# A new written-out order for TensorE's work and for the projections in the first block of a two-block attention kernel

## The chip, the cores and the metric

The kernel runs on one core of one Trainium2 chip. The metric is the device time of one execution in microseconds (us). The kernel before was timed in three runs: 1796.18, 1799.53 and 1802.74 us, median 1799.53. One execution was also taken with the hardware profiler, and every row below is from that one.

## What is computed

Two independent attention blocks, A and B, each with its own input, weights and output projection; the outputs are laid side by side. Each has 2048 tokens, width 512 and 32 heads of 16. Block A lets a token see only itself and the 255 before it; block B sees all tokens. All in float32.

```python
qkv = (x @ wqkv).reshape(B, S, 3, H, Dh)          # S=2048, D=512, H=32, Dh=16
scores = einsum("bhqd,bhkd->bhqk", q, k) * Dh ** -0.5
# block A only: keep 0 <= query - key < 256
p = softmax(scores)
o = einsum("bhqk,bhkd->bhqd", p, v) @ wo
# result: concatenate([A, B], axis=-1)
```

## The kernel before

The heads of a block are taken in 8 groups of 4, and the queries in 4 chunks of 512, so a block has 32 units (group, chunk). The two groups of a pair share a set of projected rows. For each unit the kernel finds each query's maximum score first (line 518 in block A, line 471 in block B), puts the negated maxima, split into three rounded parts, beside the queries as extra rows of the contraction, and then computes scores from which the maximum is already subtracted (line 628). ScalarE takes the exponential (line 635), GpSimd cuts the window's triangles in block A (line 645), and TensorE sums the weighted values (line 674 in block A, line 659 in block B). Sums of the weights come from a column of ones beside the values.

In the first block all 96 projections are done too: q and k of both blocks (4 pairs x 4 chunks each), and v (16 tiles of 128 tokens per block). A projection is 12 matmuls: 4 slices of the contraction, each in 3 products of a value that is split into a high and a low part. A q or k projection goes from PSUM through a buffer `st` (two of them) to DRAM (`parts`), line 324, and is loaded back by four DMAs per chunk as `oq` (line 398) or `opk` (line 382). A v projection goes through `vst` to `vd` in DRAM and back into `vt` (line 434). All these DMAs are issued by SyncE's queue (SP) in the order in which the program was written. PSUM has seven banks for all of the first block's products (one more holds the weighted sums): a projection takes one, a maximum two neighbouring ones, a score step two.

The program is laid out once, in Python, by a loop that reads a string of letters, `ORDER_A`, one letter for one piece of TensorE's work, in the order in which TensorE then executes them:

- `p`: the next projection of the list `ORDER_P`, 12 matmuls over all 128 rows of the array (line 222).
- `g`: a quarter of the next two projections of that list, their contraction cut into halves that run in two halves of the array, 12 matmuls (line 352). Four `g` make two projections.
- `m`: one item of a unit's maxima, two heads, two matmuls (line 518); in block A VectorE follows with a masked copy (line 527) and a reduction (line 528), or for the first two tiles of the sequence with two masked reductions (line 523). Eight items make a unit.
- `t`: two transposes (line 595) that bring a unit's maxima into rows; ScalarE copies them out (`ntr`, line 597), and two DMAs put them beside the queries (line 602).
- `s`: scores of one step of a unit for two heads (line 628), two exponentials. A unit has six.
- `w`: the weighted values of a step (line 674). A unit has three.
- `e`: an item of the second block's maxima that is done early (line 471).

`ORDER_P` names the projections: block, kind, and two digits; for q and k these are pair and chunk (`Aq02` is block A's queries, pair 0, chunk 2), for v they are chunk and tile of 128 in it (`Av13`). Model times in the loop decide where DMA issues and VectorE's and ScalarE's follow-up work are put between the letters; the letters themselves are never reordered. Loads of the input have conditions on how many projections have been begun (`nb`). After the last letter the second block is written by other code, with its own repeated pattern; that is not touched.

Of the kernel before, what the change touches and what calls it, by code (L numbers as in the profile page):

```python
# [48 lines left out]
FILL = 16  # L49
WARM = 22  # L50
ORDER_P = (
# [4 lines left out]
    "Bq20 Bq12 Bk30 Bk31 Bk10 Bq33 Bq30 Bq31 Bk32 Bq32 Bk33 Bk21 ").split()  # L56
WAKE = 200
GAP_V = 1500
PIECE = 4
# [4 lines left out]


ORDER_A = (
    "pppppppppppmmmmpmmgmgmptmgmgmmpmsgmsgmmpmsgmsgmwtsmgmsgmmpmsgsmgmtwwmmmpsmgmsgmswwmsgmsgmmpmssptwsmg"
    "msgmswsmgsmgmmwwmgmsgmstwmsgmsgmmwtsgmsgmswmsgmsgmswmmmpssmtwwmspmsmwssmgsmgmswtmsgsmgmwsmswssmwmmmp"
    "mtmswmsswmsmpsmmpsmwtmmmpsmswmmspmsmwsmsmwwtmsmsmsmpmsmtwsmsmwsmmswssmwmmspmmswsmwtsmgmsgmswsmgsmtgm"
    "mwsmwsmmswsmsmpsmmwmswtmsmwsmmmpmsssmmwsmsmwtmmmpsmswmsmsmwtsmsmwsmmpmmswsmtwmmmpmsgmsgmswtsmgmswpsm"  # L70
    "gsmwwmsgmmgmpmsgmsgsmwwtsmgmsgmswsmgsmgmmwtsgsmgsmwwmsgmsgmgsmgmswsmgmmgmwsmwtmsgmsgmswtmsgsmgmswwsm"
    "gmsgmswsmgsmgsmtwwmmmpmsmpmsmwsmmswtmsgmsgmswsmgsmgsmwmsmtwsmmswssmwmmmpmssmtwswmmmpmsgsmgsmwwmsgsmg"
    "etwmmmpmsgmsgmswsegsmgegesgmswsmgesgemtwmmpmsmwmswmsgsmgestwmsgesgmmpemmpmsmwwtemmpsmgmsgsmwmgegsewm"
    "mmpesstwmgmsgeswsmgsmgsmwesgsmgsmwmgsmgmswesmpsmmwtwmmmpmmmwp")
LAND = 400
LAND_V = 0
LGAP = 2500
# [1189 lines left out]
```

## Time and profile before

| | |
|---|---|
| runs | 1796.18, 1799.53, 1802.74 us (median 1799.53) |
| profiled execution, its span from first to last instruction | 1797.4 us; no other time of that execution is listed |
| TensorE (PE) busy | 1779.1 us, 99% |
| VectorE (DVE) busy | 1510.2 us, 84% |
| ScalarE (ACT) busy | 1401.6 us, 78% |
| GpSimd (POOL) busy | 651.4 us, 36% |
| first block (all letters) | 0 to about 520 us |
| second block | about 520 to 1797 us |

Times in the rows are microseconds unless marked ns. PE is TensorE's matmul side. L222 is line 222 of the kernel. Matmuls are pipelined and their ends are modelled, so the distance between the starts of two rows tells more than a row's length. In a timeline row, `x12` is the number of instructions merged, and the bracket gives idle time of the engine just before and what ended it. SPq is SyncE's queue, where a row is the issue of DMAs, not their transfer.

### The profile page before, as it was taken

How to read it: one execution, taken by the hardware profiler on the slowest of the kernel's cores; microseconds unless marked ns; L12 is line 12 of the kernel's file. 1: busy time of each engine (PE TensorE's matmuls, PEld its weight loads, DVE VectorE, ACT ScalarE, POOL GpSimd, SP SyncE). 2: the span in 40 equal slices, each digit the busy share in tenths (PEclk: the TensorE clock that was granted, in tenths of full speed). 3: DMA queues.
4: the chain of work that ended last, by engine and by line, in shares of the span. 5: the costliest groups of instructions: out<-in, count | busy, mean ns of one | idle time of the engine just before them, and what ended most of it. 6: DMA issues, size and time to landing. Idle time of an engine off the chain costs nothing.

```text
span 1797.4 us, 39182 instructions
## 1 busy us (share of the span) xinstructions
PE 1779.1 (99%) x15054; PEld 907.9 (51%) x15054; DVE 1510.2 (84%) x2244; ACT 1401.6 (78%) x2749; POOL 651.4 (36%) x1334
## 2 busy tenths in 40 slices
PE   8999999999999999999999999999999999999999
PEld 6776657767754555444444444444444444444336
DVE  4766786676789677899999999999999999999911
ACT  4366676665569677899999999999999999999983
POOL 0377888656755331133400024220112422022220
PEclk9999999999999999999999999999999999999999
DMA  7766667645562223211200310130031121010012
GB/s 256 204 204 202 202 203 224 177 143 172 187 183 87 78 86 100 52 41 37 65 17 31 72 34 29 38 70 16 17 77 35 29 64 37 17 54 9 32 37 94
DMA packets 129354, 166.80 MB, mean 93 GB/s; under 512 B 23204, under 2 KB 59044, under 8 KB 129156
## 3 DMA queue, kind: packets, MB, share of 16 engines
q1 hardware_dynamic: 129168, 164.31, 31.0%
q8 instruction: 118, 1.93, 0.4%
q14 instruction: 68, 0.56, 0.1%
HBM read 94.49 MB, written 68.19 MB: 91 GB/s over the span
## 4 chain that ended last, share of the span: by engine, by line
PE 94%; DMA 2%; ACT 1%; DVE 1%; SPq 1%; issue 1%; POOL 0%; ACTq 0%; DVEq 0%
PE ps_all L659 30%; PE ps_all L471 20%; PE ps_all L628 19%; PE ps_all L222 11%; PE ps_all L352 7%; PE ps_all L674 4%; PE ps_all L518 3%; ACT p L635 1%; DMA in<-xT_A 1%; SPq L382 0%; PE ps_all L595 0%; DVE nm L528 0%; DMA in<-xT_B 0%; DVE ps_all L527 0%; DMA vd<-vst 0%
## 5 line engine op out<-in xcount | busy, mean ns | idle before, releaser
L635 ACT ACTIVATE p<-ps_all 128x512 f32<-128x512 f32 x2432 | 1260.9, 597 | 178.8 <-PE ps_all L628 114.6
L475 DVE TENSOR_REDUCE mt<-ps_all 128x2 f32<-128x1024 f32 x1516 | 1195.6, 870 | 63.0 <-PE ps_all L471 63.0
L628 PE MATMUL ps_all<-oq,opk 51*128 51x512 f32 (+2 forms) x2752 | 768.4, 404 | 4.5 <-ACT p L635 2.4
L471 PE MATMUL ps_all<-opk,oq 48*128 48x512 f32 x2016 | 673.3, 438 | 0.2
L659 PE MATMUL ps_all<-p,vt 128*17 128x256 f32 (+1 forms) x6056 | 586.2, 460 | 1.7 <-ACT ou L685 1.7
L628 PEld LDWEIGHTS ps_all<-oq,opk 51*128 51x128 f32 x2752 | 394.6, 185 | 179.0 <-ACT p L635 150.3
L471 PEld LDWEIGHTS ps_all<-opk,oq 48*128 48x128 f32 x2016 | 307.7, 184 | 315.3 <-DVE mt L475 179.5
L645 POOL TENSOR_SCALAR_AFFINE_SELECT p<-p 128x256 f32<-128x256 f32 x480 | 179.8, 409 | 110.7 <-ACT p L635 108.8
L659 PEld LDWEIGHTS ps_all<-p,vt 128*17 128x17 f32 x6056 | 101.5, 95 | 228.1 <-issue 215.7
L545 POOL TENSOR_TENSOR mu<-mt 128x16 f32<-128x16 f32 x31 | 6.9, 221 | 509.3 <-DVE mt L475 509.3
L527 DVE COPY_PREDICATED ps_all<-mone,ps_all 128x256 f32<-128x256 uint16 x224 | 95.3, 426 | 82.0 <-PE ps_all L518 75.4
L528 DVE TENSOR_REDUCE nm<-ps_all 128x2 f32<-128x512 f32 x224 | 155.2, 693 | 7.7
L713 POOL TENSOR_TENSOR rd<-ld,minus 128x32 f32<-128x32 f32 x15 | 81.9, 5460 | 216.4 <-DMA ld<-od 216.4
L352 PE MATMUL ps_all<-x,w 64*128 64x512 f32 x720 | 119.1, 392 | 0.0
L222 PE MATMUL ps_all<-x,w 128*128 128x512 f32 x408 | 104.3, 405 | 2.9 <-ACT x L170 2.2
L674 PE MATMUL ps_all<-p,vt 128*17 128x384 f32 (+2 forms) x1408 | 94.1, 387 | 0.1
L518 PE MATMUL ps_all<-opk,oq 48*128 48x384 f32 (+2 forms) x512 | 91.8, 362 | 2.2 <-DMA oq<-parts 0.7
L222 PE MATMUL ps_all<-w_o,x_o 128*128 128x512 f32 x384 | 92.5, 395 | 0.0
L352 PEld LDWEIGHTS ps_all<-x,w 64*128 64x128 f32 x720 | 84.1, 185 | 8.8
L222 PEld LDWEIGHTS ps_all<-x,w 128*128 128x128 f32 x408 | 75.3, 191 | 25.8 <-ACT x L170 2.9
L305 ACT ACTIVATE raw<-ps_all 128x512 f32<-128x512 f32 x56 | 32.3, 597 | 70.4 <-PE ps_all L222 55.5
L222 PEld LDWEIGHTS ps_all<-w_o,x_o 128*128 128x128 f32 x384 | 70.7, 188 | 25.0 <-issue 8.4
(77 smaller groups left out, 942.2 us busy)
## 6 DMA issues: line engine op xcount, KB each, us to landing
parts<-st SPq DMA_DIRECT2D x64, 512.0 KB
oq<-parts SPq DMA_DIRECT2D x128, 128.0 KB
opk<-parts SPq DMA_DIRECT2D x128, 128.0 KB
od<-ou SPq DMA_DIRECT2D x64, 256.0 KB
vd<-vst SPq DMA_DIRECT2D x32, 272.0 KB
oq<-parts SPq DMA_DIRECT2D x128, 64.0 KB
opk<-parts SPq DMA_DIRECT2D x128, 64.0 KB
t<-od SPq DMA_DIRECT2D x32, 256.0 KB
```

Of the source, the lines that this page charges most:

```text
L222: nc.tensor.matmul(ps, l(u), r(v), start=start and k == 0, stop=stop and k == n - 1)
L352: op = nc.tensor.matmul(view(banks[a ^ turn]), l(u)[rows], r(v)[rows], start=turn == q == 0, stop=turn == 1 and q == 11)
L471: nc.tensor.matmul(ps[:, n], q[rows, 128 * qt:128 * qt + 128], k[rows, kc * QC:kc * QC + QC], start=True, stop=True)
L475: op = nc.vector.tensor_reduce(out=m[:, a:a + len(heads), r, qt, kc], in_=ps, axis=AX.X, op=ALU.max)
L518: nc.tensor.matmul(two[:, a, 0:w], opq[b, g, c][rows, r, 128 * qt:128 * qt + 128], opk2(g)[rows, r, t0:t1], start=True, stop=True)
L527: nc.vector.copy_predicated(two[:, :, 256:384], later, two[:, :, 0:128])
L528: op = nc.vector.tensor_reduce(out=m[:, :, r, qt, 0], in_=two[:, :, 128:384], axis=AX.X, op=ALU.max)
L628: nc.tensor.matmul(ps[x][:, col:col + n1], opk2(g)[rows, pr, 128 * k:128 * k + 128], opq[b, g, c][rows, pr, q0:q0 + n1], start=True, stop= ...
L635: op = nc.scalar.activation(p[:, a0 + x, :w], ps[x][:, :w], AF.Exp, scale=SCALE)
L645: nc.gpsimd.affine_select(out=v, in_=v, pattern=[[0, 2], [sign, 128]], compare_op=ALU.is_ge, fill=zero_fill, base=base, channel_multiplier ...
L659: nc.tensor.matmul(o[32 * j:32 * j + VW, q0:q1], vt[(g // 2) % 2][:, kt, vc:vc + VW], pts[1, g, c, kt, j // 2][:, j % 2, q0:q1], start=kt ...
L674: nc.tensor.matmul(o[32 * j:32 * j + VW, q0:q0 + w], vt[(g // 2) % 2][:, kt, vc:vc + VW], pts[b, g, c, m, j // 2][:, j % 2, col:col + w], ...
```

## The change

Two tables are replaced and nothing else. `ORDER_P` is a new order of the same 96 projections (the first three names are the same). `ORDER_A` is a new order of the same 761 letters: 48 `p`, 96 `g`, 280 `m`, 192 `s`, 96 `w`, 33 `t`, 16 `e` in both. All code is the same.

```diff
 ORDER_P = (
-    "Aq00 Ak00 Ak01 Av11 Av02 Av03 Aq01 Av01 Ak02 Av21 Av13 Aq02 Av12 Av00 Aq03 Ak03 Av20 Av10 Av33 Ak20 Av32 "
-    "Av23 Av22 Ak12 Av30 Av31 Ak10 Aq10 Ak11 Aq11 Ak30 Aq12 Ak13 Aq13 Ak32 Aq30 Ak31 Aq20 Ak22 Ak21 Aq21 Aq31 "
-    "Aq32 Ak33 Aq22 Ak23 Aq33 Aq23 Bq00 Bk01 Bk00 Bq02 Bk02 Bq01 Bv32 Bk03 Bv13 Bv21 Bv03 Bq03 Bv30 Bv31 Bq13 "
-    "Bv12 Bv22 Bk22 Bv00 Bq21 Bk13 Bv20 Bv11 Bk11 Bv02 Bq10 Bv10 Bk12 Bv01 Bq11 Bq23 Bk20 Bv33 Bq22 Bk23 Bv23 "
-    "Bq20 Bq12 Bk30 Bk31 Bk10 Bq33 Bq30 Bq31 Bk32 Bq32 Bk33 Bk21 ").split()
+    "Aq00 Ak00 Ak01 Av00 Av13 Av02 Aq01 Ak02 Av01 Av20 Av21 Av03 Aq02 Av10 Aq03 Ak03 Av31 Av11 Av32 Av22 Ak10 "
+    "Av12 Av23 Av30 Ak13 Av33 Aq12 Aq10 Ak12 Ak11 Ak30 Aq20 Aq11 Ak20 Aq13 Ak21 Aq21 Aq30 Ak33 Ak31 Aq22 Aq31 "
+    "Ak32 Ak22 Ak23 Aq32 Aq33 Aq23 Bk01 Bq01 Bq00 Bq02 Bq03 Bk00 Bv30 Bv10 Bv22 Bv20 Bk02 Bk03 Bv31 Bq10 Bv32 "
+    "Bv13 Bv21 Bk21 Bq22 Bv23 Bk10 Bv01 Bv33 Bq13 Bv00 Bv03 Bq20 Bv12 Bk13 Bk12 Bv11 Bk22 Bq21 Bk20 Bq11 Bv02 "
+    "Bq23 Bk23 Bk33 Bk11 Bk30 Bk32 Bq31 Bq33 Bq32 Bq12 Bq30 Bk31").split()
 ORDER_A = (
-    "pppppppppppmmmmpmmgmgmptmgmgmmpmsgmsgmmpmsgmsgmwtsmgmsgmmpmsgsmgmtwwmmmpsmgmsgmswwmsgmsgmmpmssptwsmg"
-    "msgmswsmgsmgmmwwmgmsgmstwmsgmsgmmwtsgmsgmswmsgmsgmswmmmpssmtwwmspmsmwssmgsmgmswtmsgsmgmwsmswssmwmmmp"
-    "mtmswmsswmsmpsmmpsmwtmmmpsmswmmspmsmwsmsmwwtmsmsmsmpmsmtwsmsmwsmmswssmwmmspmmswsmwtsmgmsgmswsmgsmtgm"
-    "mwsmwsmmswsmsmpsmmwmswtmsmwsmmmpmsssmmwsmsmwtmmmpsmswmsmsmwtsmsmwsmmpmmswsmtwmmmpmsgmsgmswtsmgmswpsm"
-    ...
+    "ppppppppmmpmmppmgmmgmptmgmmgmppmsgmsgmmpmsgsmgmmwtsgsmgmmpmsgmsgmwtwmmmpmsgsmgsmwwmsgmsgmmpsmsptwsmg"
+    "msgmswsmgsmgmmwtwmsgmsgmswsmgmsgmswtmgmsgsmwmgmsgmswsmmpmmstwswmmspsmwmsgmsgmswtmsgsmgmwsmsmwsmswmsm"
+    "psmmtwsmwsmmpsmmpmsmtwmmpmsswsmmpmmswtsmmswmsmswmmspsmmtwmswsmsmwmmsmswmsmpsmswtsmwsmgsmgmwsmgsmgmsw"
+    "mtmswmmswsssmmpsmmwtsmwsmmswmmmpmsswmmssmmstwmmmpmsswmmstwmsmssmmwsmpmmswtmswmmmpmsgmsgmswtmsgsmwpsm"
+    ...
```

The four lines of `ORDER_A` that are left out on each side change in the same manner.

## Rows read from the trace of the kernel before

**Rows 1.** The chain of work that ended last, shares of the span by engine.

```profile
PE 94%; DMA 2%; ACT 1%; DVE 1%; SPq 1%; issue 1%; POOL 0%; ACTq 0%; DVEq 0%
```

**Rows 2.** Busy time by stretch: length, then PE, PEld, DVE, ACT, POOL, clock, DMA.

```profile
0.00:40.00 40.00, 34.43 (x145) 26.74 (x146) 17.80 (x29) 19.26 (x33) 3.39 (x16) 0.96 0.76 254
150.00:280.00 130.00, 124.94 (x1154) 80.57 (x1148) 99.10 (x242) 89.56 (x183) 110.78 (x212) 1.00 0.64 200
40.00:520.00 480.00, 473.29 (x4395) 334.93 (x4393) 339.68 (x734) 285.83 (x575) 327.85 (x628) 1.00 0.63 192
520.00:1797.40 1277.40, 1271.38 (x10518) 546.23 (x10516) 1152.70 (x1481) 1096.52 (x2141) 320.18 (x690) 1.00 0.18 50
```

**Rows 3.** What PE waited for, 5 to 520 us: total, times, longest.

```profile
PE ps_all L628 <- ACT p L635: 2.0, 5, 0.6
PE ps_all L222 <- DVE st L312: 1.7, 1, 1.7
PE ps_all L628 <- DMA oq<-ntr: 1.2, 1, 1.2
```

**Rows 4.** PE's timeline: start, length, what, idle before.

```profile
32.10 2.88 PE L222 MATMUL ps_all<-x,w 128*128 128x512 f32 x12
34.82 2.88 PE L222 MATMUL ps_all<-w_v,x 128*128 128x512 f32 x12
39.38 3.01 PE L222 MATMUL ps_all<-w_v,x 128*128 128x512 f32 x12 [1.68 <-DVE st L312]
43.91 3.02 PE L222 MATMUL ps_all<-x,w 128*128 128x512 f32 x12
...
77.39 3.02 PE L222 MATMUL ps_all<-w_v,x 128*128 128x512 f32 x12
80.34 0.44 PE L518 MATMUL ps_all<-opk,oq 48*128 48x384 f32 x2
```

**Rows 5.** VectorE's timeline around the eleventh projection.

```profile
36.17 2.55 DVE L171 TENSOR_TENSOR x<-in,x 128x512 fp32r<-128x512 f32 x4 [5.27 <-ACT x L170]
38.64 0.68 DVE L312 TENSOR_TENSOR st<-ps_all,st 128x512 fp32r<-128x512 f32 x1
```

**Rows 6.** SP's queue: issues of the first unit's and the third unit's rows.

```profile
25.70 2.36 SPq L382 DMA_DIRECT2D opk<-parts  x4
...
43.57 1.86 SPq L382 DMA_DIRECT2D opk<-parts  x4
...
51.55 0.38 SPq L324 DMA_DIRECT2D parts<-st  x1
...
60.37 1.80 SPq L398 DMA_DIRECT2D oq<-parts  x4
```

**Rows 7.** PE's timeline, transposes and first scores of the eleventh and thirteenth units.

```profile
196.29 0.23 PE L595 MATMUL ps_all<-ident,nm 128*32 128x128 bf16 x2
...
205.77 0.70 PE L628 MATMUL ps_all<-oq,opk 51*128 51x128 f32 x4 [1.20 <-DMA oq<-ntr]
...
220.45 0.23 PE L595 MATMUL ps_all<-ident,nm 128*32 128x128 bf16 x2
...
224.56 0.34 PE L518 MATMUL ps_all<-opk,oq 48*128 48x384 f32 x2
224.74 0.39 PE L628 MATMUL ps_all<-oq,opk 51*128 51x384 f32 x4
225.06 1.06 PE L674 MATMUL ps_all<-p,vt 128*17 128x128 f32 x16
226.05 0.50 PE L628 MATMUL ps_all<-oq,opk 51*128 51x384 f32 x4
```

**Rows 8.** SP's queue, the issues of the same two units' maxima.

```profile
201.78 1.50 SPq L602 DMA_DIRECT2D oq<-ntr  x2
...
221.76 1.49 SPq L602 DMA_DIRECT2D oq<-ntr  x2
```

**Rows 9.** Busy time by stretch near the start, columns as in rows 2.

```profile
3.90:10.70 6.80, 4.15 (x20) 2.49 (x19) 3.28 (x6) 3.11 (x6) 0.30 (x2) 1.00 0.91 302
10.73:14.13 3.40, 3.40 (x9) 2.64 (x8) 3.10 (x6) 2.77 (x5) 0.00 (x0) 0.50 1.05 406
```

More of the change, by code (lines that the diff above doesn't have):

```diff
@@ L66 @@
 ORDER_A = (
-    "pppppppppppmmmmpmmgmgmptmgmgmmpmsgmsgmmpmsgmsgmwtsmgmsgmmpmsgsmgmtwwmmmpsmgmsgmswwmsgmsgmmpmssptwsmg"
-    "msgmswsmgsmgmmwwmgmsgmstwmsgmsgmmwtsgmsgmswmsgmsgmswmmmpssmtwwmspmsmwssmgsmgmswtmsgsmgmwsmswssmwmmmp"
-    "mtmswmsswmsmpsmmpsmwtmmmpsmswmmspmsmwsmsmwwtmsmsmsmpmsmtwsmsmwsmmswssmwmmspmmswsmwtsmgmsgmswsmgsmtgm"
-    "mwsmwsmmswsmsmpsmmwmswtmsmwsmmmpmsssmmwsmsmwtmmmpsmswmsmsmwtsmsmwsmmpmmswsmtwmmmpmsgmsgmswtsmgmswpsm"
[L71 to L74, printed above, removed]
+    "ppppppppmmpmmppmgmmgmptmgmmgmppmsgmsgmmpmsgsmgmmwtsgsmgmmpmsgmsgmwtwmmmpmsgsmgsmwwmsgmsgmmpsmsptwsmg"
+    "msgmswsmgsmgmmwtwmsgmsgmswsmgmsgmswtmgmsgsmwmgmsgmswsmmpmmstwswmmspsmwmsgmsgmswtmsgsmgmwsmsmwsmswmsm"
+    "psmmtwsmwsmmpsmmpmsmtwmmpmsswsmmpmmswtsmmswmsmswmmspsmmtwmswsmsmwmmsmswmsmpsmswtsmwsmgsmgmwsmgsmgmsw"
+    "mtmswmmswsssmmpsmmwtsmwsmmswmmmpmsswmmssmmstwmmmpmsswmmstwmsmssmmwsmpmmswtmswmmmpmsgmsgmswtmsgsmwpsm"
+    "gmswwmgmsgmmpmsgmsgsmwtwmsgmsgmswsmgsmgmswtmgmsgsmwwmsgmsgmgsmgmswsmgmmgmwtmswmsgsmgmstwmsgsmgmswwms"
+    "gmsgmswsmgsmgmmpmmswmstwsmmpmmswsmtwmsgsmgmswsmgsmgsmwmmstwsmmswsmswmmmpssmmwtswmmmpsmgsmgsmtwwmsgse"
+    "geswemmpmgmsgeswsmgsmgegesgmswsmgsmgmmtwmmpmsmwsmwsegsmgmswtmsgmsgmmpemmpmsmwtwemmpmsgesgsewmgmgsmwe"
+    "mmpsmstwmgesgmswsmgesgeswsegmsgsmwmgmsgmswmmspsmmpmmmwwtwmmmp")
 LAND = 400
```

## The prediction

> **What bounds the kernel now.** I read the chain of waits first: 94% of what ended last is TensorE, so time is won only where TensorE waits, or where its own work gets shorter [rows 1]. The busy times by stretch come next. The reader is to see how little is left: from 40 to 520 us TensorE is busy 473.29 of 480, idle 6.7 us; in the second block 1271.38 of 1277.40, and no code of that block is touched [rows 2]. The first 40 us have 5.6 us idle, but most of that stands before the first few projections, whose order (Aq00, Ak00, Ak01) is the same. The worst stretch is 150 to 280 us: 5.06 us idle of 130, with VectorE busy 99.10, ScalarE 89.56 and GpSimd 110.78, none of them full [rows 2]. There the engines wait for each other in turns, through the seven PSUM banks and the buffers between them. The list of TensorE's waits names three larger ones: 2.0 us in five pieces for exponentials to free a bank, 1.7 in one piece for VectorE, 1.2 in one piece for a DMA of maxima [rows 3]. The timelines then give the places of the last two.
>
> **What the change does to the work.** The letters are the same multiset, so TensorE, VectorE, ScalarE and SP have the same instructions to do. Nor does the coarse order move: I counted the letters of both strings after every hundred, and no kind differs by more than one there (after 300 letters both have 114 m, 74 s, 28 p and 36 g; after 400 both have 156, 103, 34, 39). So the load of VectorE and ScalarE per stretch is the same, and the crowded stretch at 150 to 280 us stays as crowded. What can change is local: which letters stand in a row, and how much TensorE work lies between a producer and its consumer. Four places I can price; the rest I bound.
>
> **Step 1, the start.** Before, eleven p stand first. The tenth and eleventh start at 34.82 and 39.38 where p to p otherwise takes 2.72 (32.10 to 34.82), and the row says 1.68 us idle for `st` [rows 4]. The reason is one row down: VectorE was splitting four slices of input from 36.17 to 38.72 and got to the subtraction that frees the bank only at 38.64 [rows 5]. After the change eight p stand first, then m m p m m p p m. The ninth to eleventh projections come some 1 us of maxima later, and the q/k projection whose eviction was late (Ak02) moves from ninth to eighth place, 2.72 us earlier; at about 32 us VectorE is idle and evicts it before the splits come. Four m and three p hold at most 7 banks, and the first two m are done by then. So the wait goes: -1.7. What is late next is the first m, now at about 32.1, where the eighth p ends. Its keys are issued from 25.70 to 28.06 [rows 6]; the one DMA that TensorE was seen to wait for ended 205.77 - (201.78 + 1.50) = 2.5 us after its issue was over [rows 7, 8], so they should be there at 30.6, hidden by the eighth p with 1.5 us to spare. If the four splits (2.55 us, [rows 5]) get in front of these first maxima instead, their banks come free that much later. Bounds: -1.7 to +0.8. I take -1.7, the row at this very place.
>
> **Step 2, the third unit's queries.** Aq02 is now done in a g pair, and from its end to the unit's first m there lie 3 p, 2 g, 5 m and 2 s. From rows: p to p 2.72, p to m 2.95 (77.39 to 80.34) twice, s 0.32 and m 0.18 to 0.28 [rows 4, 7], and a g at half a p's 2.72: 8.6 + 2.7 + 1.1 + 0.6 = 13.0 us. Before it was 6 g, 3 p, 12 m, 2 s and a t, some 20 us. How long does the way through DRAM take? Ak02's p began at 32.10 and ended about 35.0; its loads were issued from 43.57 to 45.43, plus 2.5: 12.9 us. Aq02's ended at 46.9, its store was issued at 51.55 and its loads from 60.37 to 62.17, plus 2.5: 17.7 us [rows 4, 6]. So bounds: 0 to +4.7. I take 0, Ak02's way: the condition that lets two weight loads into the queue (twelve projections begun) is now met by the first g, ahead of Aq02's store, and before it was met by Aq02 itself, so that they competed with that store.
>
> **Step 3, maxima on their way back.** Between a unit's t and its first s lies the copy by ScalarE and two DMAs through SP, which issues in order. At the eleventh unit the t is at 196.29, its issues end only at 203.28, 7.0 us later, and s waits 1.20 [rows 7, 8]. The new order has s m m s w m s m s w m m s p m m s m t w m between them where before it had m s m s m s m p m s m t w; that is two more w (0.99 each where a step has two pieces, 225.06 to 226.05, about half where it has one), four more m and two more s, over 2 us more: that wait goes, -1.2, if SP's queue stays as it is. (Bounds: -1.2 to 0.) The other way goes the fourteenth unit: there only m s w m m s w s s are left between, 3 x 0.25 + 4 x 0.32 + 2 x 0.99 = 4.0 us. The thirteenth unit's way is the nearest: t at 220.45, issues end at 223.25, plus 2.5 makes 5.3 us [rows 7, 8]. So +1.3; bounds 0 (if ScalarE stretches the four s anyway) and 7.0 + 2.5 - 4.0 = +5.5, if SP is as late as at the eleventh unit. No other unit has under 6 us of work between the two.
>
> **Step 4, more changes of form.** Runs of p go from 38 to 39, and runs of w and t from 86 to 87. A p before an m costs 2.95 against 2.72 before a p [rows 4]: +0.2; the run of w I put at no more than that, and take +0.2 for both (0 to +0.5).
>
> **The rest.** About 5 us of other idle time remain, in pieces of 0.2 to 0.6, five of them (2.0 us) for exponentials [rows 3]. The count of m and s around them is the same; adjacent m m go from 59 to 65, but three in a row from 16 to 8; s s from 11 to 8. Bounds: all of it gone, -5, or as much again, +5. I take 0, since the loads per stretch are the same.
>
> Sum: -1.7 + 0 - 1.2 + 1.3 + 0.2 = -1.4. Against the profiled execution that is 1797.4 - 1.4 = 1796.0. That execution lies 2.1 below the median of the runs, within their spread, so the forecast for the median is 1799.5 - 1.4 = 1798.1. A difference of 0.3% (5.4 us) is about what a measurement of this kernel can tell from no change; the forecast is within it.
>
> **Rival 1, faster: the crowded stretch loosens.** The waits of 150 to 280 us are waits in turns, and with fewer triples of m each bank pair may come free just in time. For it: no other engine is full there [rows 2]. Against it: same counts per hundred letters. If all 5.06 us of idle go (the 1.2 of step 3 is among them) and the start gains 1.7: 1799.5 - 6.8 = 1792.7; some waiting lies hidden in matmuls that are booked busy, so it could be 1789.
>
> **Rival 2, slower: rows come late through DRAM.** SP issues in order, and both tightened ways (third unit, fourteenth unit) end at a matmul behind which all of TensorE stands. At their upper ends they cost 4.7 + 5.5; with -1.7, -1.2 and +0.2 the sum is +7.5: 1807.0. It decides once the two waits together pass 8.1 us. For it: 17.7 us for Aq02's way and 7.0 for SP's delay were measured; against it: both were the worst of their kind here.
>
> The clock comes in here. Before, it fell to half in 10.73 to 14.13, after TensorE had been busy 4.15 of 6.80 us, and only nine matmuls started in those 3.40 us [rows 9]; at 0.227 each (2.72 / 12) they would have taken 2.04, so the fall cost 1.4. From 40 us on it never fell [rows 2]. The Trainium skill, "TensorE: Matmul & The Clock Gate", section "HAM oscillation", says that a wait for data between bursts sends the clock back to half rate. By that rule each of rival 2's two waits would bring a fall, and the sum would be 1807.0 + 2 x 1.4 = 1809.8; the trace agrees at the start, and shows no fall behind the 1.68 us wait.
>
> **Rival 3, nothing arrives.** Gains of the first block are given back before the second block's first step, because the last projections still have to pass VectorE and SP: 1799.5. The 1.4 us of the forecast can't be told from it.
>
> **How the numbers follow.** Forecast 0.42, rival 1 0.30, rival 2 0.18, rival 3 0.10. Faster by over 0.3% (below 1794.1): nearly all of rival 1 and a little of the forecast's tail, 0.31. Slower (above 1804.9): rival 2 and a tail, 0.19. Within: 0.50. The range takes in rivals 1 and 2: 1789 to 1807; the forecast's own is 1794.5 to 1801.5.
>
> **What would show it.** Step 1: the wait for `st` near 39 us is gone, first L518 at about 32 us, and the eleventh projection is through by about 42. Step 2: no wait for oq<-parts at the third unit's first L518. Step 3: no wait for oq<-ntr at the eleventh unit, one of about 1.3 us at the fourteenth. The rest: 150 to 280 us still has 4 to 6 us idle. The first L471 of the second block's pattern, at 520 us now, should come 1 to 2 us earlier, and 1277 us should follow as before. The prediction is wrong if the idle time in the crowded stretch falls below 2 us or a single wait of over 3 us appears.

## The result, and the profile after

The changed kernel takes 1804.04 us (median of 9 runs, 1800.62 to 1808.07), the kernel before 1799.53 (9 runs, 1796.18 to 1802.74). The ratio is 1.0028, 95% interval 1.0019 to 1.0038: slower by about 5.0 us, where 1.4 us less was forecast. The profiled execution has a span of 1806.0 us against 1797.4; its time, 1807.75 us, is the second longest of the nine and 3.7 us above their median, so its profile shows more loss than the usual execution has.

Busy time by stretch, the changed kernel (columns as in [rows 2]: the stretch and its length; after the comma the busy times of TensorE's matmuls, its weight loads, VectorE, ScalarE and GpSimd; then granted clock, DMA share, GB/s):

```profile
0.00:40.00 40.00, 35.97 (x151) 27.49 (x152) 19.39 (x40) 18.66 (x32) 3.38 (x16) 0.96 0.75 252
40.00:150.00 110.00, 107.90 (x928) 80.32 (x926) 69.25 (x154) 55.87 (x113) 57.84 (x107) 1.00 0.74 208
150.00:280.00 130.00, 125.10 (x1142) 80.58 (x1142) 94.98 (x234) 88.51 (x180) 107.34 (x209) 0.96 0.65 198
280.00:390.00 110.00, 109.93 (x1122) 80.27 (x1120) 74.41 (x175) 69.54 (x142) 74.91 (x153) 1.00 0.60 182
390.00:520.00 130.00, 129.24 (x1183) 93.06 (x1182) 98.51 (x163) 68.74 (x138) 84.63 (x161) 1.00 0.56 178
520.00:535.00 15.00, 14.42 (x90) 6.53 (x90) 10.79 (x15) 10.35 (x20) 3.68 (x4) 0.89 0.99 227
535.00:565.00 30.00, 28.79 (x240) 10.94 (x236) 27.66 (x36) 24.86 (x49) 13.32 (x27) 0.94 0.22 74
565.00:1805.00 1240.00, 1234.68 (x10213) 532.17 (x10209) 1115.21 (x1433) 1063.19 (x2078) 304.06 (x662) 1.00 0.18 48
```

The reader is to look at the busy time and the granted clock together. From 150 to 280 us TensorE is busy as before (125.10 against 124.94, [rows 2]), but the clock is 0.96. And in the first 45 us of the second block, whose code did not change, 1.79 us are idle (0.58 and 1.21) and the clock is 0.89 and 0.94. The same two stretches before have 0.20 us idle at clock 1.00:

```profile
520.00:535.00 15.00, 14.80 (x111) 6.42 (x111) 14.35 (x19) 12.47 (x24) 1.89 (x2) 1.00 0.98 225
535.00:565.00 30.00, 30.00 (x262) 12.29 (x263) 30.00 (x40) 27.30 (x54) 16.53 (x29) 1.00 0.22 73
```

Where 1.71 of those 1.79 us stand, by the timeline of the changed kernel's TensorE (only the rows with idle time before them, in brackets):

```profile
525.95 0.50 PE L628 MATMUL ps_all<-oq,opk 51*128 51x512 f32 x1 [0.50 <-ACT p L635]
557.13 0.23 PE L595 MATMUL ps_all<-ident,nm 128*32 128x128 bf16 x2 [1.21 <-POOL nm L572]
```

The second is the larger. GpSimd in front of it, the changed kernel:

```profile
550.04 0.26 POOL L552 TENSOR_SCALAR mm<-mu 128x16 f32<-128x16 f32 x1
550.26 1.28 POOL L754 TENSOR_TENSOR t<-t,bl 128x512 f32<-128x512 f32 x1
551.60 0.61 POOL L756 CAST x_o<-t 128x512 fp32r<-128x512 f32 x1
552.29 1.27 POOL L757 TENSOR_TENSOR x_o<-t,x_o 128x512 fp32r<-128x512 f32 x1
553.53 0.22 POOL L547 TENSOR_TENSOR mu<-mt,mm 128x16 f32<-128x16 f32 x1
...
556.85 0.22 POOL L572 TENSOR_TENSOR nm<-nr,nm 128x16 bf16<-128x16 f32 x1
557.03 1.28 POOL L754 TENSOR_TENSOR t<-t,bl 128x512 f32<-128x512 f32 x1
```

and the same instructions before:

```profile
545.56 0.26 POOL L552 TENSOR_SCALAR mm<-mu 128x16 f32<-128x16 f32 x1
546.69 0.22 POOL L547 TENSOR_TENSOR mu<-mt,mm 128x16 f32<-128x16 f32 x1 [0.87 <-DVE mt L475]
...
551.10 0.23 POOL L572 TENSOR_TENSOR nm<-nr,nm 128x16 bf16<-128x16 f32 x1
551.28 1.28 POOL L754 TENSOR_TENSOR t<-t,bl 128x512 f32<-128x512 f32 x1
```

An output of the first block (chunk 0, pair 1: lines 754, 756, 757, 3.3 us together) is normalised by GpSimd. In the program written before, that came behind the second block's maxima (line 572); now it stands between their first combination (line 552) and the second (line 547). GpSimd works in program order, so `nm` is done late and the transposes wait for it. The new tables shifted the model times by which the program is laid out, and that moved a piece of work in code that nobody edited.

The 0.50 us at 525.95 has another source. The two views by tile show ScalarE's four splits of the first block's output weights, changed kernel:

```profile
L170 ACT ACTIVATE w_o<-in_o x4: 622/633/644, 471.9 to 524.8; 128x512 fp32r<-128x512 f32 x4
```

and before:

```profile
L170 ACT ACTIVATE w_o<-in_o x4: 634/638/662, 470.6 to 493.6; 128x512 fp32r<-128x512 f32 x4
```

Two of these loads may begin only when all of block B's pair 1 is projected (the list of conditions `slots_of`). That pair was complete with `Bk10`, 89th of the 96 projections; in the new list it is complete with `Bq12`, the 94th. So the last split, 0.63 us, is started at 524.78, between the second block's first exponentials, and the next of these come that much later.

In the first block the changed kernel is 1.32 us ahead at 249 us (first maxima of the seventeenth unit, 248.92 against 250.24) and 3.84 us behind at 276 (275.70 against 271.86). Between the two:

```profile
253.04 0.56 PE L518 MATMUL ps_all<-opk,oq 48*128 48x256 f32 x3 [0.69 <-ACT p L635]
254.04 0.69 PE L628 MATMUL ps_all<-oq,opk 51*128 51x256 f32 x3 [0.44 <-ACT p L635]
266.19 0.74 PE L628 MATMUL ps_all<-oq,opk 51*128 51x256 f32 x8 [0.40 <-ACT p L635]
267.46 0.71 PE L518 MATMUL ps_all<-opk,oq 48*128 48x384 f32 x4 [0.53 <-ACT p L635]
```

Two pairs of short waits, 2.06 us, and behind each the granted clock goes to 0.50, half rate, for 3.4 and for 6.8 us (from 254.2 and from 267.8). The kernel before had two single waits there, and no fall:

```profile
251.58 0.55 PE L628 MATMUL ps_all<-oq,opk 51*128 51x128 f32 x3 [0.26 <-ACT p L635]
263.77 0.55 PE L628 MATMUL ps_all<-oq,opk 51*128 51x128 f32 x4 [0.59 <-ACT p L635]
```

### The profile page after: what moved, and what is told of

It is laid out like the page before. It is cut to its first block, busy times and chain, and to the rows that moved or that the text cites. A ratio compares the mean times of both kernels' runs of the same rounds, so it can differ in the third digit from the quotient of the medians.

```text
span 1806.0 us, 39182 instructions
## 1 busy us (share of the span) xinstructions
PE 1786.0 (99%) x15054; PEld 911.4 (50%) x15054; DVE 1510.2 (84%) x2244; ACT 1399.7 (78%) x2749; POOL 649.1 (36%) x1334
## 4 chain that ended last, share of the span: by engine, by line
PE 93%; DMA 3%; DVE 2%; SPq 1%; ACT 1%; POOL 0%; issue 0%; ACTq 0%; POOLq 0%; DVEq 0%
PE ps_all L659 29%; PE ps_all L471 19%; PE ps_all L628 19%; PE ps_all L222 11%; PE ps_all L352 7%; PE ps_all L674 5%; PE ps_all L518 3%; DVE mt L475 1%; DMA opk<-parts 1%; DMA parts<-st 1%; SPq L382 0%; DVE nm L528 0%; PE ps_all L595 0%; ACT p L635 0%; DMA in<-xT_A 0%
## 5 line engine op out<-in xcount | busy, mean ns | idle before, releaser
L471 PE MATMUL ps_all<-opk,oq 48*128 48x512 f32 x2016 | 675.1, 439 | 0.1
L471 PEld LDWEIGHTS ps_all<-opk,oq 48*128 48x128 f32 x2016 | 309.9, 185 | 315.6 <-DVE mt L475 179.4
L352 PE MATMUL ps_all<-x,w 64*128 64x512 f32 x768 | 124.6, 391 | 0.0
L222 PE MATMUL ps_all<-x,w 128*128 128x512 f32 x384 | 99.4, 410 | 2.5 <-ACT x L170 2.1
L352 PEld LDWEIGHTS ps_all<-x,w 64*128 64x128 f32 x768 | 89.2, 185 | 10.3
```

Of the source, the lines that this page charges most:

```text
L222: nc.tensor.matmul(ps, l(u), r(v), start=start and k == 0, stop=stop and k == n - 1)
L352: op = nc.tensor.matmul(view(banks[a ^ turn]), l(u)[rows], r(v)[rows], start=turn == q == 0, stop=turn == 1 and q == 11)
L471: nc.tensor.matmul(ps[:, n], q[rows, 128 * qt:128 * qt + 128], k[rows, kc * QC:kc * QC + QC], start=True, stop=True)
```

## The experiments

Ratios are to the kernel before, run on the same chip, with 95% intervals. A fall is a stretch of 3.4 or 6.8 us in which TensorE's granted clock is 0.50. normalise_later, bq12_early and bq12_alone take the two causes away singly and together.

**normalise_later.** GpSimd's normalise of that one output is put 5 us later in model time, behind the maxima; all else is the changed kernel.

```diff
-        after(t2, rest, ("outs", b, p, c))
+        after(t2 + 5000 * ((b, p, c) == (0, 1, 0)), rest, ("outs", b, p, c))
```

> The changed kernel, with GpSimd's normalising of chunk 0, pair 1 (three instructions, 3.3 us, around 550 us) put behind the last combination of the second block's first maxima instead of between the first and the second. Nothing else differs. Theory: in the changed kernel the transposes at 557.1 us waited 1.2 us for these three instructions and the clock then fell for 3.4 us, 2.7 us lost in all; without them in the way the time is 2 to 3 us below the changed kernel's, ratio to the kernel before about 1.001 (1.000 to 1.002). Rival (the loss is all in the first block; a late maximum has slack here): same as the changed kernel, ratio 1.0028.

Measured 1801.06 us, ratio 1.0012 (1.0001 to 1.0023). TensorE's waits from 520 to 565 us, the whole list:

```profile
PE ps_all L628 <- ACT p L635: 0.5, 1, 0.5
```

The 1.2 us is gone, the 0.5 is left. The order on GpSimd costs 0.0016 of the time, about 2.9 us, of which 1.2 is the wait seen.

**bq12_early.** The same, and `Bq12` exchanged with `Bk33`, so that pair 1 is complete at the 88th projection (`Bk11`); `Bq12` itself becomes the 87th, not the 83rd as the expectation says.

```diff
-    "Bq23 Bk23 Bk33 Bk11 Bk30 Bk32 Bq31 Bq33 Bq32 Bq12 Bq30 Bk31").split()
+    "Bq23 Bk23 Bq12 Bk11 Bk30 Bk32 Bq31 Bq33 Bq32 Bk33 Bq30 Bk31").split()
```

> As normalise_later, and in the projections' order Bq12 and Bk33 change places, so that Bq12 is the 83rd instead of the 94th or so (it was the last of its pair, and two loads of the output projection's weights wait for the pair). Theory: the late loads put ScalarE's splits of these weights (0.63 us each) between the first exponentials of the second block, and a wait of 0.5 us and a fall of the clock at 527 us follow, 1.8 us; with Bq12 early the splits come before 515 us and this goes as well: 1 to 2 us below normalise_later, ratio to the kernel before 0.9995 to 1.001. Rival: the clock falls there anyway because the second block starts thinly; no difference to normalise_later.

Measured 1799.54 us, ratio 1.0000 (0.9991 to 1.0010). The list of waits from 520 to 565 us is empty, as before the change, and the four splits now stand from 467.9 to 480.7 us. Repeated on another chip (bq12_early_2, below) the ratio is 1.0007 (0.9994 to 1.0021). So nearly all of the loss goes when two pieces of work outside the letters are put in their old order, and of the new order without them no effect can be told from none.

The wait of 0.5 us is gone, but the fall of the clock there is not; the rival's mechanism holds. In bq12_early's profile (stretches of 4.1 and 3.4 us):

```profile
519.50:523.60 4.10, 3.90 (x21) 2.09 (x25) 3.67 (x6) 3.40 (x7) 1.09 (x1) 1.00 0.95 173
523.60:527.00 3.40, 3.40 (x18) 0.98 (x14) 2.48 (x4) 1.61 (x4) 0.00 (x0) 0.50 1.06 174
```

Of the 14 profiles of this case, four have the wait of 0.5 us, and two of these a fall behind it (after, back_new). Ten do not have it, and five of these have a fall that begins between 522 and 530 us (bq12_early, front_new, front_k03, k03_later, middle_old), with no wait in the list from 518 to 532. So a fall there cannot be put down to the late split.

**bq12_alone.** The exchange without the shift of the normalise.

> The changed kernel with Bq12 and Bk33 exchanged in the projections' order, and nothing else (GpSimd's normalising stays in front of the maxima). Theory (late splits of the output weights cost time of their own at the second block's start): 1 to 2 us below the changed kernel, ratio to the kernel before 1.0015 to 1.0022. Rival (they cost 0.2 us, what the trace of normalise_later shows between the second block's steps 1 and 3: 5.06 us against 4.87 before; the rest of the 1.5 us between normalise_later and bq12_early is scatter): ratio 1.0025 or more.

Measured 1802.34 us, ratio 1.0016 (1.0006 to 1.0026); the waits from 520 to 565 us:

```profile
PE ps_all L595 <- POOL nm L572: 1.2, 1, 1.2
```

With 1.0028 (neither mended), 1.0012, 1.0016 and 1.0000 (both) the two effects add up: 0.0016 for the normalise and 0.0012 for `Bq12`, each found in two comparisons, 2.9 and 2.2 us. From the intervals of the four ratios each size is good to some 0.0010, 1.8 us; which wait belongs to which edit is sharp.

**front_new, back_new.** The new tables up to the 48th projection and the 332nd letter and the old behind, and the other way round (the edit is shown in short).

```diff
 # front_new
+ORDER_P = new[:48] + old[48:];  ORDER_A = new[:332] + old[332:]
 # back_new
+ORDER_P = old[:48] + new[48:];  ORDER_A = old[:332] + new[332:]
```

> The first 332 letters and 48 projections of the new order (to about 248 us), the rest from the old order. Theory (the loss is made behind 248 us: two falls of the clock at 254 and 268 us, one at 527, one at 558): the new front is worth -1.3 us and the rest is as before, ratio 0.9985 to 1.0005. Rival (the loss is in the front, in the waits at 59 to 63 us for the third unit's loads): ratio 1.001 to 1.003.

> The first 332 letters and 48 projections of the old order, the rest from the new one. Theory (the loss is made behind 248 us): the loss of the changed kernel and a little more, since the front's gain is missing: ratio 1.0025 to 1.004. Rival (the loss is in the front): ratio 0.999 to 1.001.

Measured 1800.03 us, ratio 1.0007 (0.9998 to 1.0016), and 1803.15 us, ratio 1.0018 (1.0006 to 1.0030). Both waits behind 520 us (0.5 and 1.2) are in back_new, none is in front_new. Most of the loss goes with the later half of the tables; of the front half no effect can be told from none. Not all that back_new's profile loses is the later half's, though: in it the old start waits 2.75 us for `st` at 40.5 us, where the kernel before waited 1.68 [rows 4], and a fall follows.

**k03_later, front_k03.** These go for step 2. By 62 us ScalarE stands before an eviction. TensorE has two waits at that time, and the second is for the exponentials behind that eviction; for the first, before the first scores, the trace names no releaser (changed kernel, ScalarE, then TensorE):

```profile
56.16 0.60 ACT L301 ACTIVATE st<-ps_all 128x512 fp32r<-128x512 f32 x1 [2.02 <-PE ps_all L222]
62.39 0.60 ACT L301 ACTIVATE st<-ps_all 128x512 fp32r<-128x512 f32 x1 [5.64 <-DMA parts<-st]
62.89 1.08 ACT L635 ACTIVATE p<-ps_all 128x512 f32<-128x512 f32 x2
```

```profile
60.20 0.59 PE L628 MATMUL ps_all<-oq,opk 51*128 51x384 f32 x3 [0.99 <-issue]
63.53 0.93 PE L628 MATMUL ps_all<-oq,opk 51*128 51x384 f32 x3 [1.06 <-ACT p L635]
```

`Aq02`, `Aq03` and `Ak03` now follow each other through the two `st` buffers; the third eviction waits for the first to be stored, and in ScalarE's queue the first exponentials stand behind it. The edit, made in bq12_early and in front_new, exchanges `Ak03` and `Av31`:

```diff
-... Aq02 Av10 Aq03 Ak03 Av31 Av11 ...
+... Aq02 Av10 Aq03 Av31 Ak03 Av11 ...
```

> bq12_early with Ak03 and Av31 exchanged in the projections' order, so that Aq02, Aq03 and Ak03 no longer follow one another through the two st buffers. Theory: ScalarE's eviction of Ak03 (at 62.4 us, after 5.6 us of waiting for the store of Aq02) stood in front of the first exponentials, and TensorE waited 0.5 to 1.0 and 1.1 us for them at 60 and 63 us; these waits go: 1.5 to 2 us below bq12_early, ratio to the kernel before 0.9985 to 0.9995. Rival (the loads of the third unit's queries come no earlier, so the wait moves to its first maxima): same as bq12_early, ratio 1.000.

> front_new (new order to letter 332, old behind it) with Ak03 and Av31 exchanged as in k03_later. Theory: the waits of 2.8 us for the first scores at 61 us go, 2 to 2.5 us below front_new's 1.0007: ratio 0.9990 to 0.9998. Rival (the wait moves on): ratio 1.0005 to 1.001.

Measured 1803.16 us, ratio 1.0019 (1.0010 to 1.0029), and 1806.00 us, ratio 1.0037 (1.0024 to 1.0050): both some 0.002 to 0.003 slower than without the exchange. ScalarE's wait for the store is gone, and TensorE's of 1.06 us with it. The wait before the first scores is still there, 1.43 us in k03_later and 1.68 in front_k03, so it was not ScalarE's stand; and other waits come. SyncE's queue of k03_later, where a row is an issue:

```profile
63.20 5.23 SPq L398 DMA_DIRECT2D oq<-parts  x8
68.86 5.64 SPq L426 DMA_DIRECT2D vd<-vst  x2
...
77.73 2.11 SPq L398 DMA_DIRECT2D oq<-parts  x4
80.30 1.71 SPq L382 DMA_DIRECT2D opk<-parts  x4
```

and TensorE:

```profile
68.93 0.68 PE L518 MATMUL ps_all<-opk,oq 48*128 48x384 f32 x2 [0.78 <-DMA oq<-parts]
...
84.75 0.41 PE L518 MATMUL ps_all<-opk,oq 48*128 48x384 f32 x1 [1.39 <-DMA opk<-parts]
```

SyncE is held at two stores of `vst` from 68.86 to 74.50 (in bq12_early, without the exchange, they stand apart, at 69.73 and 73.40, and four loads of keys are issued between them), and the loads behind it are late: rival 2's mechanism, in miniature. The gain of the theories did not come, and the loss is larger than the rivals had it.

**k03_raw.** The other cure, in bq12_early: `Ak03` goes into a row buffer and GpSimd splits it, so that ScalarE need not wait for an `st`.

```diff
-        if (b, p) == (0, 0):
+        if (b, p) == (0, 0) and (s, c) != (1, 3):
             op = nc.scalar.activation(two[:, 0], ps, AF.Copy)
```

> bq12_early (both causes behind the first block mended) with one eviction more changed: Ak03 goes from PSUM into a row buffer (line 305) and GpSimd splits it, as all other pairs do, so that ScalarE does not wait for the third `st`. Theory (the stand of ScalarE is step 2's cost): ScalarE's wait of 5.2 us before that eviction and TensorE's 1.1 us at 63.3 go, the third unit's first L518 comes at about 68.0 instead of 69.1, and the median is 1.0 to 1.5 us below bq12_early's ratio of 1.0000 (0.9991 to 0.9996). Rival (the time only moves on, as with k03_later): Ak03 is stored later, its four loads push SP, and TensorE waits 1 us or more for oq or opk at 69 or 84 us: ratio 1.000 or above.

Measured 1800.39 us, ratio 1.0007 (0.9997 to 1.0018). As the theory has it up to 82 us: ScalarE's wait and both of TensorE's are gone, and the third unit's maxima start at 66.75 us, earlier even than the 68.0 expected. Then it is lost in a place that nobody named:

```profile
94.71 3.10 PE L674 MATMUL ps_all<-p,vt 128*17 128x384 f32 x24 [2.01 <-DMA vt<-vd]
```

A fall follows at 94.9 us. So the rival's ratio, with a wait for a DMA of values instead of queries or keys. The time saved by 62 us has now been lost again behind three kinds of loads.

**scores_twice.** bq12_early, with the score matmuls of the second block's first unit issued twice in its first three steps, into the same bank (the second writes the same values over the first); this keeps TensorE busy where ScalarE is late.

```diff
-                nc.tensor.matmul(ps[x]..., start=True, stop=True)
+                for _ in range(2 if (b, g, c) == (1, 0, 0) and kt < 3 else 1):
+                    nc.tensor.matmul(ps[x]..., start=True, stop=True)
```

> bq12_early with every score matmul of the first three steps of the second block issued twice into the same bank (24 matmuls more, about 2.5 us of TensorE's time by their distance of 0.1 us in pairs). Theory: the clock falls at 523 to 527 us in four of six profiles because TensorE works thinly there while the first exponentials fill the pipeline; with the repeats it does not fall, the repeats lie partly in idle time, and the time is within 1 us of bq12_early, ratio 0.9995 to 1.0005. Rival (the fall comes from what was done before, or the repeats only delay): the fall stays in the profile, and the ratio is 1.001 or more.

Measured 1800.61 us, ratio 1.0008 (0.9999 to 1.0016). From 520 to 535 us TensorE is busy 15.00 of 15.00 us at clock 1.00, where bq12_early had 14.80 and 0.89. The median does not follow. The mean granted clock of its 11 executions is 0.9975, of bq12_early's 11 it was 0.9977, so over all executions no falls were saved that the record could show; one profile without a fall does not decide between theory and rival.

**after_again.** The changed kernel, profiled once more.

> The changed kernel once more, for its profile alone. Theory (the places of TensorE's clock falls in 200 to 300 us are not fixed by the program): the falls at 254 and 268 us do not both return at these places, while the waits by 557 us for `nm` (1.2 us) and by 63 us for ScalarE (1.06 us) do, within 0.2 us. Rival (the new order fixes them): falls within 1 us of 254.2 and 267.8, and the first block again ends 5 us later behind 280 us than its waits alone explain.

One execution: 1803.80 us, span 1802.1. Neither side holds whole. The clock falls at 61 (7 us long) and at 269, not at 254; no fall at 527 or 558. The waits return, 0.51 at 526.04 and 1.23 at 555.78, but the one at 63 us is 0.29 instead of 1.06, inside a fall. And the first block ends where it did, at 521.27 us against 521.19 (518.27 before): behind the start both executions have some 10.2 us of half clock in that block, in different places. This execution is 0.2 us from the changed kernel's median. Its span is 4.7 us longer than before, 3.0 of it in the first block and 1.7 in the second, which is the two waits and no more. The program fixes these two waits; it does not fix where a fall comes.

**middle_old, bq12_early_2.** bq12_early with the letters 328 to 377 as before, and bq12_early once more beside it.

```diff
-"...mmmpmsswmmssmmstwmmmpmsswmmstwmsmssmmwsmpmmswtmsw..."
+"...mmmpmsssmmwsmsmwtmmmpmsswmsmsmwtsmsmwsmmpmmswsmtw..."
```

> bq12_early with the 50 letters 328 to 377 (some 234 to 265 us) put back in the order of before; both stretches hold the same letters. Theory (the new order's two pairs of waits there, 0.69 + 0.44 and 0.40 + 0.53 us for exponentials, cost their 2.1 us against 0.85 before, and bring a fall of TensorE's clock in most executions): the pairs are gone, in their place 0.2 to 0.6 once or twice, no fall in 250 to 275 us, and the time is 1 to 3 us below that of bq12_early_2 on the same chip (ratio 0.9985 to 0.9995). Rival (the waits are only passed on, as at the start): waits of about 2 us return within 30 us behind 265, ratio as bq12_early_2's.

> bq12_early once more, beside middle_old on the same chip. Both theories: ratio 1.0000, from 0.9990 to 1.0010. For the falls of the clock: theory, one in 250 to 275 us in the profiled execution (it was without one the first time, where six of the seven other executions with these letters had one or more); rival, none there again, and then the order of these letters does not set them.

Measured 1801.34 us, ratio 0.9997 (0.9983 to 1.0012), and 1800.46 us, ratio 1.0007 (0.9994 to 1.0021). The ratios differ as the theory has it, the medians the other way; the intervals overlap nearly whole: inconclusive. The theory's step failed: the waits did not shrink, five of them stand in middle_old from 249 to 264 us (0.26, 0.37, 0.74, 0.63, 0.58, together 2.58 us against 2.03 in bq12_early_2), yet without a fall. bq12_early_2 had one at 267; of the eight other executions with these letters up to then seven had one, not six of seven. No kernel tried here beats the one before.

## Why the prediction was wrong, step by step

**The second block is the step that failed.** The prediction took it as a cost that stays ("no code of that block is touched", "1277 us should follow as before"). The tables put 1.7 us of waits there, 0.50 for ScalarE and 1.21 for GpSimd; both are in after, after_again and back_new, and each goes with the edit that puts its piece of work back. With both edits the ratio falls from 1.0028 to 1.0000, and to 1.0007 on another chip, so some 3.8 to 5.0 us go. The code was untouched, but the tables set the model times and the places by which it is laid out. Both could have been followed in the program: the normalise by its due time against that of the maxima, and `Bq12`'s place by the conditions of the `w_o` loads. The prediction followed the loads of the start only.

**The clock is the term that the sum did not have.** The waits are 1.7 us of the 5.0. The prediction had falls in one sentence on rival 2, and none in the forecast. The record has the mean granted clock of each execution, and the time goes with it. The changed kernel took 1800.62 us at 0.997 and 1808.07 at 0.992; a straight line through its nine executions gives 1.4 us for every 0.001, and one fall of 3.4 us lowers that mean by 0.0009. For the kernel before, 102 executions beside the experiments give 1.4 too (on average 1797.1 us at 1.000 and 1804.5 at 0.995). Their mean clock is 0.9978, the changed kernel's 0.9952. By that line the difference is worth some 3.6 us, an estimate that is good to some 1.6. With the waits of 1.7, and less the 1.3 by which the changed kernel is ahead at 249 us, that makes 4.0, inside the measured 3.4 to 6.8.

The two edits bring the clock back as well: 0.9961 in normalise_later, 0.9972 in bq12_alone, 0.9977 and 0.9966 with both. But the profiles do not show the falls behind the waits that the edits remove. In the changed kernel's first profile each of the two is followed by one, which makes 4.3 us between 523 and 562 us (1.74 by 532, 2.73 from 549 on, some 0.2 won back between); the wait for `nm` is in four profiles, and only this one has a fall behind it. Why falls are more frequent stays open.

**Step 1 was right in its number, and not in its reason.** The wait for `st` is gone, and the first maxima came at 32.6 us:

```profile
32.62 0.32 PE L518 MATMUL ps_all<-opk,oq 48*128 48x128 f32 x1
33.20 0.41 PE L518 MATMUL ps_all<-opk,oq 48*128 48x128 f32 x3 [0.26 <-DMA opk<-parts]
33.53 3.03 PE L222 MATMUL ps_all<-w_v,x 128*128 128x512 f32 x12
36.49 0.50 PE L518 MATMUL ps_all<-opk,oq 48*128 48x256 f32 x4
36.93 5.73 PE L222 MATMUL ps_all<-w_v,x 128*128 128x512 f32 x24
```

Where 1.68 us stood at 39.38 [rows 4] there is one unbroken row of 24 matmuls, which ends the eleventh projection by 42.6; a wait of 0.26 for the keys, which were to be there with 1.5 us to spare, is what came late next. But the reason was that VectorE would take `Ak02` out of its bank at about 32 us, before the splits of the input. ScalarE's copy of it is at 32.72, and VectorE's subtraction still stands between the splits (36.24 and 38.05):

```profile
37.45 0.68 DVE L312 TENSOR_TENSOR st<-ps_all,st 128x512 fp32r<-128x512 f32 x1
```

That is 1.2 us earlier than before [rows 5], not over 6. So TensorE had other work while that bank was held, four maxima between the projections; that these made the wait go is argued, not tested, and the step's full gain is in part luck.

**Step 2 was right on what it priced and missed what stands beside it.** The third unit's first maxima do not wait for their queries: 0, as taken. But they start at 69.19 against 67.73, 1.46 later, because TensorE had waited 0.99 and 1.06 us by 60 and 63 us, the second time behind ScalarE's stand. The step followed `Aq02` through SyncE and DRAM and not through ScalarE and the two `st` buffers. By the fourth unit some 0.3 is left, and the experiments could not win it back.

**Step 3 was right in its gain and too dark in its loss.** The eleventh unit no longer waits for its maxima, though three more m lie between and not four, and though SyncE was slower: the issues ended 9.7 us after the transposes (193.68 to 203.40), where 7.0 was taken, and the scores came at 205.05. The fourteenth was to wait 1.3 us and does not: its transposes are at 230.76, its DMAs are issued from 231.59 to 233.06, and its first scores at 234.88 find the rows there. 4.1 us of work lie between, as counted, but SyncE was free 0.8 us after the transposes, and the rows landed within 1.8 us of the issue where 2.5 were taken.

**Step 4 and the sum.** At 249 us the changed kernel is 1.32 us ahead. That this is nearly the sum of 1.4 is in part luck: step 3's loss of 1.3 did not come, and the two waits by 60 and 63 us, which no term held, did. The two pairs of waits by 253 and 266 us then take that and more. These were "the rest": the prediction put 0 there, with bounds of -5 and +5, "since the loads per stretch are the same". The idle time of 150 to 280 us did stay (4.90 against 5.06); what was not reckoned with is that the clock can fall behind such pieces. So neither of the prediction's own signs of being wrong came (idle time below 2 us there, or a wait of over 3). Its sign for the second block did: the first L471 of that block stands at 523.04 against 520.12, 2.9 us later and not 1 to 2 earlier. One smaller slip: the 2.1 us by which the profiled execution was to lie below the median compares a span with times; a time is some 1.7 us longer than its span (1807.75 and 1806.0 here), and the sum does not hang on it.

**The rivals.** None of them happened as told. Rival 2 had the sign, and its time (1807.0) is nearer than the forecast's, but no wait of its two places came. Its sentence on the clock bears on what did. Of the ten profiled executions with the new letters at 250 to 275 us, eight have a fall there (bq12_early and back_new have none); of the four with the old letters there (before, front_new, front_k03, middle_old), one. The Trainium skill, "TensorE: Matmul & The Clock Gate", section "HAM oscillation", ties such falls to waits for data between bursts. The pairs agree with it in kind, though in that section's case a wait is some 3 to 5 us and here the longest is 0.69. But the wait of 1.23 us at 555.78 in after_again was followed by none, five waits in middle_old were followed by none, and five falls by 522 to 530 us had no such wait before them.

## What to carry to other kernels

Where a table sets model times or places in a list, its effect ends where those times are last read, not where the table's own work ends: look up every in-order queue and every load condition behind the edit, GpSimd's above all, before a block is booked as unchanged. A wait removed from a chain of small buffers and in-order queues tends to reappear at the next queue; price the next one too. Judge a change of 0.1 to 0.3% by medians of many runs, and use a single profile to find waits, not to add up the time. Compare the mean granted clock of the executions too: here it held more of the loss than the waits did.

## What the runs showed of the hardware

The falls of TensorE's clock to half are not a property of the program alone. Two profiles of the same kernel (after, after_again) have them at 12, 254, 268, 527, 558 and 1735 us, and at 10, 61 and 269; bq12_early at 11 and 523, bq12_early_2 at 11, 267 and 1728. Behind the start most begin where TensorE has just waited, 0.5 to 2.8 us in all, but five, between 522 and 530 us, begin with no wait listed and TensorE busy for 3.90 or 3.91 of the 4.10 us before; the kernel before and four others pass the same place at full clock. They last 3.4 or about 7 us. A fall of 3.4 us cost about 1.4 us at the start of the kernel before [rows 9], and the line through the executions gives 1.4 us for 0.001 of mean clock. In the trace, bq12_early_2, with one of 3.4 us more than bq12_early in the first block, was 0.30 us ahead of it at 249 us (249.07 against 249.37) and ended that block 0.76 us later (518.31 against 517.55).
